# Late attention as one run of products per tile, with a compact state, in a fused attention, gate and expert kernel

## The chip, the cores and the metric

One core of one Trainium2 chip runs the kernel. The metric is the device time of one execution in microseconds; three runs of the kernel before gave 864.8 to 867.6, with a median of 867.41. A difference under about 0.3% (2.6 us) can't be told from none.

## The reference

Three parts follow one another. The sizes are 4 batches, 8 heads, 768 steps, head width 64; 3072 tokens of width 512; 768 columns in the first expert layer; 8 experts of 1024 columns.

```python
gamma = 1.0 - 2.0 ** (-5.0 - np.arange(H))
for t in range(S):                                    # attention: a decaying state per head
    state = gamma * state + outer(k[t], v[t])
    y[t] = q[t] @ state / sqrt(D)
h = np.maximum(np.maximum(x @ w1, x @ w2), x @ w3)    # x: all tokens, heads side by side
x = h @ w_out
logits = x @ w_gate                                   # each expert takes its 384 best tokens
out[mask_e] = np.maximum(x[mask_e] @ w1[e], 0) @ w2[e]
```

## The kernel before

Attention works on 24 tiles of 128 steps. `ORDER` goes through the batches first, so four neighbouring tiles are one block of 512 tokens, and there are six blocks. Within a tile the recurrence is written as products: scores (keys by queries, `pa`, `scores`, L216), masked on VectorE into `at` (L230); the state by the queries into `px` (L242); keys by values into `pp`, which is added to the state (L247, L259); values by masked scores into `px` as well (L250). ScalarE copies `px` into `xhi`, rounded to a shorter format, and VectorE puts the rest into `xlo` (L260, L261), so that later products are made of three products in that format. `visit` (L232) does this for tile t and calls `scores` for tile t+1 at its end.

Heads lie in pairs: heads 2j and 2j+1 share one product's 128 rows. The state is a tile of 128 by 4 by 128 per batch, with the two heads' 64 by 64 squares on the diagonal and zeros beside them, cleared by GpSimd at the start (L408); its product has all 128 rows and columns, four of them per tile.

`att_front` (L176) brings a tile there: SP loads queries, keys and values (`load_tile`, two tiles ahead), GpSimd multiplies in the decay (L186), and then queries and keys are transposed. For the first eight tiles (`DIRECT = 8`) TensorE does that (L194). For the late ones VectorE transposes squares of 32 by 32 (`blocks`, L204), and SP moves them out to memory and back in place (`there`, L206, and `qk`, L208); ScalarE then copies the keys to `kT` (L212). The buffers of `qk` are two, so the way back for tile t+2 begins when tile t's products have read theirs.

`moe1` (L347) makes the wide products `pm` of 128 by 512 (L358): for each of 18 groups (six parts of the columns, three matrices) twelve products, and ScalarE or VectorE takes the maximum into `hb`. `logits` (L372) multiplies `hb` by the product of the output and gate weights, 24 products of 32 columns per block, in three runs of 16, 4 and 4 products. These have the bank `pl`, `px` has one, the wide products three, and the pool `att` three.

All of it is written as generators. `interleave` (L110) advances the attention of the next block by so many steps per step of `moe1`; a late tile's front has five yields. A scheduler then orders each engine's instructions along these lines, so the order on the chip is close to that of the code, not equal to it. In the first part of the program block 0 and block 1 go through the first matrix alone, while the weights of the others are loaded and decoded from 64-bit numbers on VectorE (`decode`, L291 to L295), rounded on ScalarE (L309) and split on GpSimd (L310). After the sixth block the tokens are multiplied by the output weights (`x2`, L485) while the routing is worked out, and then the eight experts run (L801, L814); their products `py` alternate between the banks `px` and `pl`.

Of the kernel before, what the change touches and what calls it, by code (L numbers as in the profile page):

```python
# [23 lines left out]
P = 128  # L24
# [102 lines left out]
HALF = (slice(0, 64), slice(64, 128))  # L127


class Kernel:  # L130
    def __init__(self, ctx, tc, q, k, v, w1, w2, w3, w_out, w_gate, e1, e2, ca, cr, out):
# [17 lines left out]
        self.tiles, self.fronts, self.ats = {}, {}, {}  # L149
# [4 lines left out]
    def bank(self, tag, shape, bufs, name):  # L154
        return self.ps.tile(shape, F32, tag=tag, name=name, bufs=bufs)
# [10 lines left out]
    def load_tile(self, t):  # L166
        if t >= NT or t in self.tiles:
            return
        b, c = ORDER[t]
        self.tiles[t] = []  # L170
        for n, src, bufs in (("q", self.q, 2), ("k", self.k, 4), ("v", self.v, 4)):
            x = self.sp.tile([P, H, D], F32, tag="in_" + n, name="in_" + n, bufs=bufs)
            self.nc.sync.dma_start(x, src[b, :, c * P:(c + 1) * P, :].rearrange("h t d -> t h d"))
            self.tiles[t].append(x)

    def att_front(self, t):  # L176

# [6 lines left out]
        of_tile = lambda n: ca[:, CA["t" + n]].rearrange("p (c h) -> p c h", h=H)[:, ORDER[t][1]]  # L184
        for n, x in (("q", qn), ("k", kn)):
            nc.gpsimd.tensor_tensor(x, x, of_tile(n).unsqueeze(2).to_broadcast([P, H, D]), op=OP.mult)  # L186
# [28 lines left out]

    def scores(self, t):  # L216
# [5 lines left out]
        for j in range(4):  # L222
            for g in range(2):
                nc.tensor.matmul(pa[g][:, j].rearrange("p (b i) -> p b i", b=4),
                                 kT[HALF[g], j].rearrange("p b i -> p (b i)"), qT[HALF[g], :, j, :],
                                 start=j == 0, stop=True, skip_group_check=True)
        mask = self.ca[:, CA["mask"]].unsqueeze(1).to_broadcast([P, 4, P])
        self.ats[t] = [self.ap.tile([P, 4, P], F32, tag="at", name="at") for _ in range(2)]
# [3 lines left out]
    def visit(self, t, xhi, xlo, off):  # L232
# [6 lines left out]
        px = self.bank("px", [P, 4, P], 1, "px")  # L239
        if c > 0:  # L240
            for j in range(4):
                nc.tensor.matmul(px[:, j, :].rearrange("p (b i) -> p b i", b=4), state[:, j, :], qT[:, :, j, :],  # L242
                                 start=j == 0, stop=False, skip_group_check=True)
        if c < CPB - 1:
            pp = self.bank("att", [P, 4, 64], 3, "pp")
            for h in range(H):
                nc.tensor.matmul(pp[HALF[h % 2], h // 2, :], ks[:, h, :], vt[:, h, :], start=h < 2, stop=True,  # L247
                                 skip_group_check=True)
        for h in range(H):
            nc.tensor.matmul(px[HALF[h % 2], h // 2, :], vt[:, h, :], at[h % 2][:, h // 2, :],  # L250
                             start=c == 0 and h < 2, stop=True, skip_group_check=True)
# [8 lines left out]
        nc.scalar.copy(xhi[:, :, off:off + P], px)  # L260
        nc.vector.tensor_tensor(xlo[:, :, off:off + P], px, xhi[:, :, off:off + P].bitcast(F32), op=OP.subtract)  # L261

    def att_block(self, i, x):
        if i == 0:
            yield from self.att_front(0)
            yield from self.att_front(1)
            self.scores(0)
            yield
        for b in range(B):
            t = i * B + b  # L270
            self.visit(t, *x, b * P)
            if t + 2 < NT:
# [74 lines left out]
    def moe1(self, i, x, hb, only=None, tail=None):  # L347
# [5 lines left out]
        for n, (f, w) in enumerate(groups):  # L353
# [13 lines left out]
            if tail and n in (12, 13, 16):  # L367
                next(tail)
# [3 lines left out]
    def logits(self, i, hb):  # L372
# [3 lines left out]
        pl = self.bank("pl", [P, B, 32], 1, "pl")  # L376
# [7 lines left out]
        yield  # L384
        for f in range(4):
            product(f)
        yield
        product(4)
        yield
        product(5)  # L390
# [5 lines left out]
    def phase_ab(self, ctx_h):  # L396
# [3 lines left out]
        with ExitStack() as ctx:  # L400
# [20 lines left out]
            fill = chain(self.att_block(2, xn), self.logits(0, hbs[0]))  # L421
            interleave(self.moe1(1, x, hbs[1], only=(1, 2)), fill, 24 / 24)
            for i in range(2, NB):
                x, hbs[i] = xn, new_h()
                fill, tail = [], None
                if i + 1 < NB:
                    xn = new_x()
                    fill.append(self.att_block(i + 1, xn))
                else:
                    tail = self.logits(i, hbs[i])  # L430
                fill = chain(*fill, self.logits(i - 1, hbs[i - 1]))
                interleave(self.moe1(i, x, hbs[i], tail=tail), fill, 24 / 36)
# [357 lines left out]
    def ffn(self, e):  # L790
# [16 lines left out]
        for g in range(3):  # L807
            py = self.bank(("px", "pl")[g % 2], [P, DM], 1, "py")
# [82 lines left out]
```

## Time and profile before

| | us |
|---|---|
| median of three runs | 867.41 |
| the profiled execution, its own time | 867.75 |
| its span, first to last instruction | 866.0 |
| TensorE busy | 830.4 (96%) |
| VectorE busy | 412.4 (48%) |
| ScalarE busy | 224.2 (26%) |
| GpSimd busy | 271.8 (31%) |
| wide products of `moe1` (L358), 1296 | 518.8 |

TensorE's busy time is a union of the products' durations, which overlap: a wide product is listed with 0.40 us, though the next one starts about 0.23 after it. A busy engine in this sense is one that always has a product under way, and its price per product is the distance between starts. A product in the 32-bit format leaves two records in the trace, one in the shorter format a single record. The granted clock of TensorE is 1.00 at 2.4 GHz and 0.50 at 1.2 GHz; its mean over the span is 0.978.

### The profile page before, as it was taken

The numbers are of one execution on the slowest core, as the hardware profiler recorded it, in microseconds if no ns is written. First come the engines' busy times: TensorE is split into PE (matmuls) and PEld (weight loads), VectorE is DVE, ScalarE is ACT, GpSimd is POOL, SyncE is SP. The second block draws the span as 40 slices with busy tenths as digits, with TensorE's granted clock in tenths as the row PEclk, the third lists the DMA queues.
The fourth block names the chain that finished last, engine by engine and source line by source line (L and its number), as shares of the span: only waits on it lengthen the run. The fifth ranks groups of instructions, "written<-read, shape, count | busy, mean of one in ns | idle before, by whom it ended". The sixth has DMA issues, their size and how long they took to land. (4 is left out here: it accounts for less than half of the span.)

```text
span 866.0 us, 13113 instructions
## 1 busy us (share of the span) xinstructions
PE 830.4 (96%) x5210; PEld 692.1 (80%) x5210; DVE 412.4 (48%) x727; ACT 224.2 (26%) x360; POOL 271.8 (31%) x275
## 2 busy tenths in 40 slices
PE   7997999999999999999999999989899998989997
PEld 6775888878878878877777777678789888888996
DVE  3687483544334322231149766746355544446310
ACT  3433211101111111211024223144244433344210
POOL 5565031111110100002026555356444743515001
PEclk9898999999999999999999999999899999989999
DMA  9979485657446413100037654149657756452000
GB/s 221 208 193 222 128 262 175 159 171 169 111 133 170 134 38 124 47 27 1 1 115 251 206 169 149 50 124 229 149 150 200 179 164 179 129 171 67 13 24 37
DMA packets 129342, 118.02 MB, mean 136 GB/s; under 512 B 82048, under 2 KB 106752, under 8 KB 128256
## 3 DMA queue, kind: packets, MB, share of 16 engines
q1 hardware_dynamic: 123232, 96.54, 41.5%
q0 software_dynamic: 5328, 14.16, 5.3%
q10 hardware_dynamic: 720, 6.47, 1.9%
q8 instruction: 41, 0.67, 0.3%
q14 instruction: 21, 0.17, 0.1%
HBM read 88.30 MB, written 28.84 MB: 135 GB/s over the span
## 5 line engine op out<-in xcount | busy, mean ns | idle before, releaser
L358 PE MATMUL pm<-xhi,whi 128*128 128x512 f32 x432 | 176.2, 409 | 5.3 <-ACT xhi L260 5.3
L358 PE MATMUL pm<-xlo,whi 128*128 128x512 f32 x432 | 171.3, 397 | 0.5 <-DVE xlo L261 0.5
L358 PE MATMUL pm<-xhi,wlo 128*128 128x512 f32 x432 | 171.3, 396 | 0.0
L762 POOL DMA_INDIRECT xg<-x_rows,idx x87 | 95.7, 1100 | 102.8 <-DVE xt L777 69.7
L365 DVE TENSOR_TENSOR hb<-hb,pm 128x512 f32<-128x512 f32 x72 | 49.5, 687 | 163.1 <-PE pm L358 160.0
L462 POOL TENSOR_TENSOR hsl<-hb,hsh 128x256 fp32r<-128x256 f32 x72 | 61.6, 886 | 152.8 <-ACT hsh L460 149.6
L358 PEld LDWEIGHTS pm<-xhi,whi 128*128 128x128 f32 x432 | 81.8, 190 | 28.3 <-ACT xhi L260 5.5
L750 DVE TENSOR_TENSOR elo<-eraw,ehi 128x1024 fp32r<-128x1024 f32 x64 | 78.9, 1245 | 41.6 <-ACT ehi L749 23.6
L358 PEld LDWEIGHTS pm<-xhi,wlo 128*128 128x128 f32 x432 | 81.5, 189 | 19.1
L358 PEld LDWEIGHTS pm<-xlo,whi 128*128 128x128 f32 x432 | 81.6, 189 | 18.6 <-DVE xlo L261 1.4
L801 PE MATMUL ph<-xtlo,ehi 128*128 128x384 f32 x256 | 88.8, 347 | 5.3 <-issue 5.2
L801 PE MATMUL ph<-xthi,ehi 128*128 128x384 f32 x256 | 89.2, 350 | 2.7 <-issue 1.6
L801 PE MATMUL ph<-xthi,elo 128*128 128x384 f32 x256 | 88.5, 346 | 1.8 <-issue 1.7
L749 ACT CAST ehi<-eraw 128x1024 fp32r<-128x1024 f32 x64 | 65.7, 1049 | 45.4 <-PE py L814 18.1
L814 PE MATMUL py<-elo,hhi 128*128 128x512 f32 x192 | 74.9, 390 | 0.0
L814 PE MATMUL py<-ehi,hlo 128*128 128x512 f32 x192 | 74.8, 390 | 0.0
L814 PE MATMUL py<-ehi,hhi 128*128 128x512 f32 x192 | 74.7, 389 | 0.0
L805 DVE SCALAR_TENSOR_TENSOR hlo<-ph,hhi 128x384 fp32r<-128x384 f32 x64 | 35.3, 555 | 59.2 <-ACT hhi L804 54.4
L485 PE MATMUL px<-wohi,hsh 128*128 128x512 f32 x144 | 58.8, 408 | 0.6 <-PEq L593 0.6
L363 ACT COPY hb<-pm 128x512 f32<-128x512 f32 x36 | 21.1, 587 | 147.0 <-PE pm L358 147.0
L186 POOL TENSOR_TENSOR in_k<-in_k,ca 128x512 f32<-128x512 f32 x24 | 26.2, 1093 | 102.6 <-DMA in_k<-in_k_dram 90.0
L485 PE MATMUL px<-wolo,hsh 128*128 128x512 f32 x144 | 57.0, 396 | 0.0
(155 smaller groups left out, 1189.3 us busy)
## 6 DMA issues: line engine op xcount, KB each, us to landing
eraw<-in_moe_w_dram SPq DMA_DIRECT2D x36, 512.0 KB
eraw<-in_moe_w_dram SPq DMA_DIRECT2D x112, 128.0 KB
w<-in_moe_w_dram SPq DMA_DIRECT2D x24, 384.0 KB
there<-blocks SPq DMA_DIRECT2D x16, 512.0 KB
qk<-there SPq DMA_DIRECT2D x64, 128.0 KB
in_q<-in_q_dram SPq DMA_DIRECT2D x24, 256.0 KB
in_k<-in_k_dram SPq DMA_DIRECT2D x24, 256.0 KB
in_v<-in_v_dram SPq DMA_DIRECT2D x24, 256.0 KB
```

Source lines behind the costliest of these rows:

```text
L186: nc.gpsimd.tensor_tensor(x, x, of_tile(n).unsqueeze(2).to_broadcast([P, H, D]), op=OP.mult)
L358: nc.tensor.matmul(pm, a[w][kt][:, f * P:(f + 1) * P], xx[:, kt, :], start=m == 0, stop=m == 3 * KD - 1)
L363: nc.scalar.copy(hb[:, f, :], pm)
L365: nc.vector.tensor_tensor(hb[:, f, :], hb[:, f, :], pm, op=OP.max)
L462: nc.gpsimd.tensor_tensor(lo[:, f:f + 2, :], hb[:, f:f + 2, c * P:(c + 1) * P], hi[:, f:f + 2, :].bitcast(F32), op=OP.subtract)
L485: nc.tensor.matmul(pm, a[:, f, :], self.wo[f][b], start=m == 0, stop=m == 3 * NF - 1)
L749: nc.scalar.copy(hi, raw)
L750: nc.vector.tensor_tensor(lo, raw, hi.bitcast(F32), op=OP.subtract)
L762: nc.gpsimd.indirect_dma_start(out=x[:, b * P:(b + 1) * P] if e else x, out_offset=None, in_=self.x2_rows.rearrange("n (r c) -> (n r) c", ...
L801: mm = nc.tensor.matmul(pm, a[:, kt, :], x[:, kt, :], start=m == 0, stop=m == 3 * KD - 1)
L805: nc.vector.scalar_tensor_tensor(hlo[f], pm, 0.0, hhi[f].bitcast(F32), op0=OP.max, op1=OP.subtract)
L814: mm = nc.tensor.matmul(py, a[:, s], b, start=m == 0, stop=m == 3 * KF2 - 1)
```

## The change

- The state becomes 128 by 4 by 64 per batch: the heads are paired as j and j+4, one in the upper and one in the lower 64 rows, and there are no zeros to clear. Its product is eight products of 64 rows by 64 columns; `px` has two banks, one for each half of the rows, and `pl` goes. Logits take a bank of `att`; so do the experts' `py`.
- From tile 8 on a visit begins with the scores of the next tile, and all its products are tied in the written order (`follow`). In the early tiles the scores still end the visit.
- The logits of blocks 0 to 4 are one run of 24 products, for blocks 0 to 3 right behind the second visit of a block.
- Of tile 8's front only the first step is done between the visits of tiles 6 and 7; its transposes, its scores and then tile 9's front follow tile 7's visit.
- The steps per step of `moe1` are 20 for 24 or 36 instead of 24.
- Queries and keys of the first eight tiles are loaded in two halves of the heads; late transposes on VectorE come in four halves instead of two.

```diff
-    def keep_warm(self, x, n, tag="pl"):
+    def keep_warm(self, x, n, tag="px"):
...
+            if n != "v" and t < DIRECT:
+                for g in range(2):
+                    self.nc.sync.dma_start(x.rearrange("p (j g) d -> p g j d", g=2)[:, g], src[:, 4 * g:4 * g + 4])
...
-                nc.vector.transpose(blocks[:, :, n], x.rearrange("p h d -> p (h d)").rearrange("p (j r d) -> p r j d", j=4, r=4))
+                x = x.rearrange("p (r j) (e d) -> p r e j d", r=2, e=2)
+                for r in range(2):
+                    nc.vector.transpose(blocks[:, 2 * r:2 * r + 2, n], x[:, r])
...
+    def follow(self, mm):
+        if self.behind:
+            self.tc.add_manual_dep(mm.ins, self.behind.name, NEXT, reason="kinds of products together")
+        self.behind = mm.ins
...
-        px = self.bank("px", [P, 4, P], 1, "px")
+        px = self.ps.tile([P, 2, 512], F32, tag="px", name="px", bufs=1)[:, :, :2 * P]
+        out = lambda h: px[HALF[h % 2], h // 4, h % 4 // 2 * P:(h % 4 // 2 + 1) * P]
+        steady, ahead = t >= DIRECT, t + 1 in self.fronts
+        self.behind = None
+        if steady and ahead:
+            self.scores(t + 1)
         if c > 0:
-            for j in range(4):
-                nc.tensor.matmul(px[:, j, :].rearrange("p (b i) -> p b i", b=4), state[:, j, :], qT[:, :, j, :],
-                                 start=j == 0, stop=False, skip_group_check=True)
+            for h in (0, 4, 1, 5, 2, 6, 3, 7):
+                g, j = h // 4, h % 4
+                self.follow(nc.tensor.matmul(out(h).rearrange("p (b i) -> p b i", b=4), state[HALF[g], j, :],
+                                             qT[HALF[g], :, j, :], start=j < 2, stop=True, skip_group_check=True))
...
-        if t + 1 in self.fronts:
+        if not steady and ahead:
             self.scores(t + 1)
-        if c < CPB - 1:
-            for r in HALF:
-                if c == 0:
-                    nc.scalar.copy(state[r, :, r], pp[r])
-                else:
-                    nc.vector.tensor_tensor(state[r, :, r], pp[r], state[r, :, r], op=OP.add)
+        if c == 0:
+            nc.scalar.copy(state, pp)
+        elif c < CPB - 1:
+            nc.vector.tensor_tensor(state, pp, state, op=OP.add)
...
-    def att_block(self, i, x):
+    def att_block(self, i, x, beside=None, at=1):
...
+            self.visit(t, x, b * P)
+            if beside and b == at:
+                for _ in beside:
+                    pass
+            if t == DIRECT - 2:
+                first = self.att_front(t + 2)
+                next(first)
+                yield
+            elif t == DIRECT - 1:
+                yield from first
+                self.scores(t + 1)
+                self.behind = None
+                yield from self.att_front(t + 2)
...
-        pl = self.bank("pl", [P, B, 32], 1, "pl")
+        pl = self.bank("att", [P, B, 32], 3, "pl")
...
-            self.states = [self.wp.tile([P, 4, P], F32, name=f"state{b}") for b in range(B)]
-            for state in self.states:
-                nc.gpsimd.memset(state, 0.0)
+            self.states = [self.wp.tile([P, 4, 64], F32, name=f"state{b}") for b in range(B)]
...
-            fill = chain(self.att_block(2, xn), self.logits(0, hbs[0]))
-            interleave(self.moe1(1, x, hbs[1], only=(1, 2)), fill, 24 / 24)
+            fill = self.att_block(2, xn, self.logits(0, hbs[0]))
+            interleave(self.moe1(1, x, hbs[1], only=(1, 2)), fill, 20 / 24)
...
-            py = self.bank(("px", "pl")[g % 2], [P, DM], 1, "py")
+            py = self.bank("att", [P, DM], 3, "py")
```

How the order of the instructions changes is shown at three places. In these rows the first word is the line of the code, `x8` says that eight such instructions follow one another, and the sizes are those of the output. The first place is TensorE around the visit of tile 9 (its state is `state_158`; L242, L247, L250 and L224 are state, keys by values, values by scores, and scores of tile 10). Before:

```order
L358 MATMUL pm<-xlo,whi_583 128x512
L358 MATMUL pm<-xhi,wlo_587 128x512
L242 MATMUL px<-qk,state_158 128x128 x4
L247 MATMUL pp<-in_v,in_k 64x64 x8
L250 MATMUL px<-at,in_v 64x128 x8
L224 MATMUL pa<-qk,kT 128x128 x8
L358 MATMUL pm<-xhi,whi_580 128x512
```

Now (L245, L271, L276, L279, and L425 for the logits, which before stood elsewhere in three runs):

```order
L403 MATMUL pm<-xlo,whi_589 128x512
L403 MATMUL pm<-xhi,wlo_593 128x512
L245 MATMUL pa<-qk,kT 128x128 x8
L271 MATMUL px<-qk,state_158 64x128 x8
L276 MATMUL pp<-in_v,in_k 64x64 x8
L279 MATMUL px<-at,in_v 64x128 x8
L425 MATMUL pl<-hb,wpr 32x128 x24
L403 MATMUL pm<-xhi,whi_586 128x512
```

The scores went from the end of the run to its start, the state's products are eight of half the rows and half the columns, and block 0's logits follow the visit in one run.

The second place is TensorE around the visit of tile 7 (`state_160`), the last tile of block 1. Before, the wide products behind it are already block 1's, which need this tile:

```order
L358 MATMUL pm<-xlo,whi_244 128x512
L358 MATMUL pm<-xhi,wlo_248 128x512
L242 MATMUL px<-qk,state_160 128x128 x4
L247 MATMUL pp<-in_v,in_k 64x64 x8
L250 MATMUL px<-at,in_v 64x128 x8
L358 MATMUL pm<-xhi,whi_241 128x512 x3
```

Now the wide products within the visit, and 16 behind it, are still block 0's:

```order
L271 MATMUL px<-qk,state_160 64x128 x8
L276 MATMUL pp<-in_v,in_k 64x64 x8
L279 MATMUL px<-at,in_v 64x128 x2
L403 MATMUL pm<-xhi,whi_243 128x512
L403 MATMUL pm<-xlo,whi_243 128x512
L403 MATMUL pm<-xhi,wlo_247 128x512
L403 MATMUL pm<-xhi,whi_244 128x512
L403 MATMUL pm<-xlo,whi_244 128x512
L403 MATMUL pm<-xhi,wlo_248 128x512
L403 MATMUL pm<-xhi,whi_245 128x512
L403 MATMUL pm<-xlo,whi_245 128x512
L279 MATMUL px<-at,in_v 64x128 x6
```

The visit moved ahead by 16 wide products, and eight more split its last kind, of which the first two need the first half of the mask and the six behind them the second.

The third place is VectorE at the same visit, from the first half of tile 7's mask on. `w` is a raw piece of weights, `wbits` its decoded form. Before:

```order
L230 TENSOR_TENSOR at<-pa,ca 128x512
L295 SCALAR_TENSOR_TENSOR wbits<-w_719,wbits 128x384
L291 TENSOR_SCALAR wbits<-w_721 128x384
L230 TENSOR_TENSOR at<-pa,ca 128x512
L293 SCALAR_TENSOR_TENSOR wbits<-w_721,wbits 128x384
L204 STREAM_TRANSPOSE blocks<-in_k 128x4x128
L295 SCALAR_TENSOR_TENSOR wbits<-w_721,wbits 128x384
L291 TENSOR_SCALAR wbits<-w_800 128x384
```

Now (piece 730 answers to 719 before, 732 to 721):

```order
L251 TENSOR_TENSOR at<-pa,ca 128x512
L338 SCALAR_TENSOR_TENSOR wbits<-w_703,wbits 128x384
L336 TENSOR_SCALAR wbits<-w_730 128x384
L340 SCALAR_TENSOR_TENSOR wbits<-w_703,wbits 128x384
L336 TENSOR_SCALAR wbits<-w_732 128x384
L338 SCALAR_TENSOR_TENSOR wbits<-w_730,wbits 128x384
L338 SCALAR_TENSOR_TENSOR wbits<-w_732,wbits 128x384
L340 SCALAR_TENSOR_TENSOR wbits<-w_730,wbits 128x384
L340 SCALAR_TENSOR_TENSOR wbits<-w_732,wbits 128x384
L251 TENSOR_TENSOR at<-pa,ca 128x512
L287 TENSOR_TENSOR state_160<-pp,state_160 128x256
L219 STREAM_TRANSPOSE blocks<-in_q 128x2x128
```

All of the decoding of pieces 730 and 732 now stands ahead of the second half of the mask, where before two steps of the last piece stood behind it; the first half of the mask stands further ahead.

## Rows read from the trace of the kernel before

**Rows 1.** Stretches: length, PE, PEld, DVE, ACT, POOL busy, PE clock, DMA share, GB/s.

```profile
0.00:70.00 70.00, 62.23 (x612) 52.38 (x614) 46.40 (x78) 27.05 (x52) 38.80 (x42) 0.95 0.89 202
...
77.00:84.00 7.00, 6.52 (x20) 4.67 (x21) 4.99 (x8) 1.62 (x3) 5.02 (x5) 0.70 1.19 261
...
95.00:139.00 44.00, 43.96 (x236) 35.93 (x234) 29.71 (x49) 7.53 (x17) 12.59 (x15) 1.00 0.60 177
139.00:444.00 305.00, 305.00 (x2113) 245.17 (x2112) 101.57 (x170) 37.94 (x64) 29.51 (x33) 1.00 0.37 100
```

**Rows 2.** TensorE's timeline at tile 9: start, duration, line, names, records.

```profile
151.45 1.05 PE L242 MATMUL px<-qk,state 128*128 128x128 f32 x8
152.44 0.69 PE L247 MATMUL pp<-in_v,in_k 128*64 128x64 f32 x16
152.95 1.05 PE L250 MATMUL px<-at,in_v 128*64 128x128 f32 x16
153.93 1.16 PE L224 MATMUL pa<-qk,kT 64*128 64x128 f32 x16
155.02 0.51 PE L358 MATMUL pm<-xhi,whi 128*128 128x512 f32 x1
...
162.10 0.38 PE L242 MATMUL px<-qk,state 128*128 128x128 f32 x2
```

**Rows 3.** TensorE's timeline at block 0's logits.

```profile
184.88 1.08 PE L380 MATMUL pl<-hb,wpr 128*32 128x128 f32 x32
185.90 0.50 PE L358 MATMUL pm<-xhi,whi 128*128 128x512 f32 x1
...
187.47 0.43 PE L380 MATMUL pl<-hb,wpr 128*32 128x128 f32 x8
187.83 0.50 PE L358 MATMUL pm<-xhi,whi 128*128 128x512 f32 x1
```

**Rows 4.** TensorE's timeline, second and last of 36 wide products between logits.

```profile
431.24 0.51 PE L358 MATMUL pm<-xhi,whi 128*128 128x512 f32 x1
431.58 0.39 PE L358 MATMUL pm<-xlo,whi 128*128 128x512 f32 x1
...
439.49 0.40 PE L358 MATMUL pm<-xhi,wlo 128*128 128x512 f32 x1
439.81 0.43 PE L380 MATMUL pl<-hb,wpr 128*32 128x128 f32 x8
```

**Rows 5.** TensorE's timeline at tile 20, whose visit has no keys by values.

```profile
328.20 1.09 PE L250 MATMUL px<-at,in_v 128*64 128x128 f32 x16
329.23 0.49 PE L224 MATMUL pa<-qk,kT 64*128 64x128 f32 x4
```

**Rows 6.** TensorE's timeline behind tile 7's visit.

```profile
76.75 1.65 PE L358 MATMUL pm<-xhi,whi 128*128 128x512 f32 x3 [5.27 <-ACT xhi L260]
78.88 0.80 PE L358 MATMUL pm<-xlo,whi 128*128 128x512 f32 x1 [0.48 <-DVE xlo L261]
```

**Rows 7.** ScalarE's timeline: the split of tile 7.

```profile
76.12 0.58 ACT L260 CAST xhi<-px 128x512 fp32r<-128x512 f32 x1
```

**Rows 8.** VectorE's timeline around tile 7.

```profile
61.89 0.43 DVE L259 TENSOR_TENSOR state<-pp,state 64x256 f32<-64x256 f32 x1
...
68.50 0.68 DVE L230 TENSOR_TENSOR at<-pa,ca 128x512 f32<-128x512 f32 x1
69.10 1.24 DVE L293 SCALAR_TENSOR_TENSOR wbits<-w,wbits 128x384 int32<-128x384 int32 x1
70.26 0.70 DVE L204 STREAM_TRANSPOSE blocks<-in_k 128x512 f32<-128x512 f32 x1
70.89 0.51 DVE L295 SCALAR_TENSOR_TENSOR wbits<-w,wbits 128x384 int32<-128x384 int32 x1
...
78.13 0.69 DVE L261 TENSOR_TENSOR xlo<-px,xhi 128x512 fp32r<-128x512 f32 x1
```

**Rows 9.** ScalarE's timeline: keys of tile 10 come back from memory.

```profile
149.17 0.62 ACT L212 COPY kT<-qk 128x512 f32<-128x512 f32 x1 [5.18 <-DMA qk<-there]
```

More of the change, by code (lines that the diff above doesn't have):

```diff
@@ L148, in __init__ @@
         self.wo_rows = self.dp.tile([FF, DM], F32, name="wo_rows")
-        self.tiles, self.fronts, self.ats = {}, {}, {}
+        self.tiles, self.fronts, self.ats, self.behind = {}, {}, {}, None
         self.zeros = self.cp.tile([P, P], BF16, name="zeros")
@@ L154, in bank @@
     def bank(self, tag, shape, bufs, name):
+        if tag == "px":
+            return self.ps.tile([P, 2, 512], F32, tag=tag, name=name, bufs=1)[:, 0, :shape[1]]
         return self.ps.tile(shape, F32, tag=tag, name=name, bufs=bufs)
-    def keep_warm(self, x, n, tag="pl"):
+    def keep_warm(self, x, n, tag="px"):
         pw = self.bank(tag, [P, 512], 1, "warm")
@@ L223, in scores, with visit @@
             for g in range(2):
-                nc.tensor.matmul(pa[g][:, j].rearrange("p (b i) -> p b i", b=4),
-                                 kT[HALF[g], j].rearrange("p b i -> p (b i)"), qT[HALF[g], :, j, :],
-                                 start=j == 0, stop=True, skip_group_check=True)
+                self.follow(nc.tensor.matmul(
+                    pa[g][:, j].rearrange("p (b i) -> p b i", b=4), kT[HALF[g], j].rearrange("p b i -> p (b i)"),
+                    qT[HALF[g], :, j, :], start=j == 0, stop=True, skip_group_check=True))
         mask = self.ca[:, CA["mask"]].unsqueeze(1).to_broadcast([P, 4, P])
-        self.ats[t] = [self.ap.tile([P, 4, P], F32, tag="at", name="at") for _ in range(2)]
+        self.ats[t] = [self.ap.tile([P, 4, P], F32, tag="at", name="at", bufs=4) for _ in range(2)]
         for at, p in zip(self.ats[t], pa):
             nc.vector.tensor_tensor(at, p, mask, op=OP.mult)
-    def visit(self, t, xhi, xlo, off):
+    def visit(self, t, x, off):
         nc = self.nc
@@ new lines, in visit @@
+        for h in (0, 1, 4, 5, 2, 3, 6, 7):
+            self.follow(nc.tensor.matmul(out(h), vt[:, h, :], at[h // 4][:, h % 4, :], start=c == 0 and h % 4 < 2, stop=True,
+                                         skip_group_check=True))
+        if not steady and ahead:
+            self.scores(t + 1)
+        self.behind = None
[3 more added lines that the diff above has]
+            nc.vector.tensor_tensor(state, pp, state, op=OP.add)
+        px = px.rearrange("p g (j i) -> p g j i", j=2)
@@ L264, in att_block @@
+        xhi, xlo = [a[:, :, off:off + P].rearrange("p (g j) i -> p g j i", g=2) for a in x]
+        nc.scalar.copy(xhi, px)
+        nc.vector.tensor_tensor(xlo, px, xhi.bitcast(F32), op=OP.subtract)
+    def att_block(self, i, x, beside=None, at=1):
         if i == 0:
@@ L267, in att_block @@
             self.scores(0)
+            self.behind = None
             yield
@@ L270, in att_block @@
             t = i * B + b
-            self.visit(t, *x, b * P)
-            if t + 2 < NT:
+            self.visit(t, x, b * P)
[9 more added lines that the diff above has]
+                self.scores(t + 1)
+                self.behind = None
+                yield from self.att_front(t + 2)
+            elif t + 2 < NT:
                 yield from self.att_front(t + 2)
@@ L367, in moe1, with logits @@
             if tail and n in (12, 13, 16):
-                next(tail)
+                next(tail, None)
         if i < NB - KEPT and (only is None or 2 in only):
             nc.scalar.dma_start(self.h_rows[i], hb)
-    def logits(self, i, hb):
+    def logits(self, i, hb, stops=()):
         nc = self.nc
-        pl = self.bank("pl", [P, B, 32], 1, "pl")
+        pl = self.bank("att", [P, B, 32], 3, "pl")
         def product(f):
@@ L382, in product @@
                                  skip_group_check=True)
-        yield
-        for f in range(4):
+        for f in range(NF):
+            if f in stops:
+                yield
             product(f)
[L387 to L390, printed above, removed]
         lt = self.lp.tile([P, B, 32], F32, tag="lt", name="lt")
```

33 lines of the change are left out of this document (17 added, 16 removed).

## The prediction

> **What bounds the kernel now.** I read the busy time by stretch first, because a share over the whole span hides which stage is full. In the stretch from 139 to 444 us TensorE is busy for 305.00 of 305.00 us at the full clock of 2.4 GHz, with VectorE at 101.6 and the DMA engines at 0.37 [rows 1]. Nothing is waited for there: what TensorE issues is what the stretch lasts, and a microsecond of issue saved is a microsecond of the end. From 95 to 139 it is busy for 43.96 of 44. Only the first 77 us have holes. Second I read TensorE's timeline, by start times: the duration of a product there overlaps with the next one, so the price of a run is the distance from its start to that of the next kind. Third, VectorE's and ScalarE's timelines at tile 7, where the largest hole lies.
>
> **One late visit.** Before, tile 9 takes from 151.45 to 155.02, that is 3.57 us: the old state's product 0.99 (8 records for 4 products), keys by values 0.51, scores by values 0.98, scores of the next tile 1.09 [rows 2]. To this comes what a change of the array's shape costs the wide products around it. Wide products start every 0.2326 us (34 steps from the second to the 36th in 7.91 us) [rows 4]; 30 of them between two visits take 7.08, 0.10 over 30 times the pitch [rows 2], and 36 between two pieces of the logits 8.57, 0.20 over [rows 4]. So 0.10 is the first wide product behind a narrow run, and the other 0.10 is the entry from a wide product into a narrow shape. The old state product has the wide shape, so a visit enters free; now it begins with the scores, which fill half the rows, and pays. Before: 3.57 + 0.10 = 3.67.
>
> The state product is now eight products of 64 rows by 64 columns, 16 records in four quarters of the array. No row of the trace has that shape. The bounds: with two at a time it is what scores by values take for as many records, 0.98 [rows 2]; with four at a time it is the logits' price, which put four products side by side: 32 records take 1.02 and 8 take 0.36, or 0.0275 a record, so 16 take 0.58 [rows 3]. I take 0.58, since the row halves (scores) and the column quarters (logits) overlap each by itself and the new order goes round the quarters. It also changes shape twice inside narrow runs instead of once; such a change shows as 0.05 more, 1.03 for scores by values right behind the state product at tile 20 [rows 5] against 0.98 behind keys by values [rows 2]. After: 0.10 + 1.09 + 0.05 + 0.58 + 0.51 + 0.98 + 0.10 = 3.41, which is 0.26 less. Sixteen visits (tiles 8 to 23): **4.2 us**. On the price of overlap the Trainium skill (TensorE: Matmul & The Clock Gate, "Measured speedup vs the span model") says that each further tile of the array adds some 4 ns to one product; four rounds would then take about 0.48 and 16 visits 1.6 us less still, an estimate by that page that no row here shows and the sum does not use. The same notes speak against the change elsewhere (TensorEngine Tiling, "Key Properties"): another tiling mode drains the engine. The 0.10 and 0.05 above are what such a change costs in this trace, and the visit has one more of them now.
>
> **The logits.** Before, a block's logits are three runs of 32, 8 and 8 records with wide products between: 1.02 + 0.36 + 0.36, an entry of 0.10 and a first wide product of 0.10, and 0.17 for each stretch between (six wide products take 1.57, their pitch is 1.40) [rows 3]: 2.28. Now 48 records stand in one run, 1.02 + 16 x 0.0275 = 1.46. Behind a visit (blocks 0 to 3) they pay only a change of 0.05, so 0.77 less each; block 4's stand alone, 1.46 + 0.20, 0.62 less. Block 5's keep their three stops. Together **3.7 us**.
>
> **Tile 7.** Before, tile 7's visit comes when all 72 wide products of block 0's first matrix are done. The next wide product needs that tile: it starts at 76.75 after an idle 5.27, released by ScalarE's split, and another waits 0.48 more for VectorE's [rows 6]. The split itself is short; it stood in ScalarE's queue behind casts of decoded weights until 76.12 [rows 7], and VectorE's half behind the decoding until 78.13 [rows 8]. In the change tile 7's visit comes four steps earlier, and the order of TensorE puts 16 wide products of block 0 behind it. They cover the split. What is late next is the second half of tile 7's masked scores: it started at 68.50 before and now has two decoding steps more ahead of it (1.24 and 0.51), and fewer: three second halves of a state sum at 0.43 and half of a transpose of 0.70 [rows 8]. That gives 68.6 to start; VectorE is at work nearly all the time there, yet every earlier TensorE step gives it some of its idle time back, so I take 68.6 for its end, 0.7 earlier. Then six products by values (0.73 at 0.061 a record), 0.10, and 16 x 0.2326 = 3.72: block 1's first wide product at 73.2 instead of 76.75, and no wait of 0.48, since VectorE needs behind the mask one state sum, three half transposes, a decode step and the split, 2.6 to 3.6 us, against 4.6 on TensorE. Gain **4.1 us**. Ends: the mask no earlier, 3.4; VectorE quick enough that it is not waited for, 6.2. The clock was at 0.70 on the mean from 77 to 84 us [rows 1], so for 4.2 us it ran at 1.2 GHz, behind that idle time, and lost 2.1. A wait of some 3 us for the mask stays, so I count no gain of clock; the other end is 2.1.
>
> **What costs nothing.** Late transposes on VectorE come in four halves instead of two of 0.70 [rows 8], between 0 and 1.4 us more per tile, 22 at most; 139 to 444 has 203 idle [rows 1]. Of 16 more load issues on SP in the first 62 us (queries and keys of tiles 0 to 7 in two halves) the bytes are the same, and the DMA engines are at 0.89 there [rows 1], so bytes set the pace; without that cover each would delay the loads behind it. GpSimd's four clears of the state and ScalarE's second state copies go, beside longer waits. The products y alternate over three banks of the common pool instead of two of their own, with one bank more to evacuate. SP's transpose loads wait for the state product (it reads the last of a tile), now 1.2 us later in the run. Before, keys of tile 10 were ready at 149.79 [rows 9], 1.66 ahead of tile 9's visit; the visit is now 36 products behind the last instead of 30, 1.4 later, so the slack stays at about 1.9, and more where 54 lie between. Behind 444 us nothing changes place; it moves as a whole.
>
> **The sum.** 4.2 + 3.7 + 4.1 = 12.0 us. The profiled execution took 867.75 for a span of 866.0, 0.3 over the median of 867.41; from the median this gives **855.4 us**.
>
> **The rivals.** (a) The hole at tile 7 stays: VectorE decodes at its pace, the new order only moves the wait from the split to the mask, and block 1 starts at 76.75 again. For it speaks how full VectorE is; against it that 24 wide products now stand where TensorE stood still. Only 7.9 are gained: 859.5. (b) The quarters run only two at a time, since every quarter shares its rows with one and its columns with another. The state run takes 0.98, each late visit 0.40 more: 855.4 + 6.4 = 861.8. Against it: both kinds of sharing overlap by themselves. (c) Slower: quarters don't overlap at all. Then 16 records at the 0.124 of the old run take 1.98, 1.40 over my price, 22.4 in all: 877.8. It turns into a loss from 1.33 us a run on (12.0 over 16, plus 0.58). No row speaks for it, none excludes it. (d) The scores, now first in the run, wait for their keys: each microsecond by which these come late is paid at 15 visits, so that 0.8 eats the gain and 1.0 gives 855.4 + 15 = 870.4. The slack of 1.9 stands against it.
>
> **How the numbers follow.** The forecast, with the ends above (the clock kept, no wait at the mask, a cheaper or dearer change of shape), spans 849 to 858.5 and gets 0.62; (a) 0.17, (b) 0.13, (c) 0.04, (d) 0.04. The range from 848.5 to 862 takes in the first three and leaves out (c), (d) and the cases where (a) and (b) meet. A measurement of this kernel can tell about 0.3%, 2.6 us. Faster by more than that are the forecast, (a) and (b) but for the 0.04 in which they add up to nothing: 0.88. Within it that 0.04 and half of (d): 0.06. Slower: 0.06.
>
> **What would show it.** In the profile after: 16 state records from start to next kind in 0.55 to 0.65, a run from scores to the next wide product in 3.3; 48 logits records in 1.4 to 1.5 right behind a visit; TensorE full from 95 to the end of the blocks, and that stretch shorter by 8; block 1's first wide product at 72 to 74 us, behind a wait of about 3 us inside tile 7's visit. A state run of 0.9 or more is (b) or (c); an idle TensorE ahead of the scores, released by keys, is (d); block 1's start at 76 or later is (a). Wrong altogether would be a stretch behind 444 us that changes its length by more than 2 us.

## The result, and the profile after

The changed kernel takes **853.7 us** (median of four runs, 852.3 to 860.6) beside 867.5 for the kernel before on the same chip: ratio **0.9877**, 95% interval 0.984 to 0.991. (The quotient of the two medians is 0.984, at the edge of that interval.) Run again later, beside other kernels, it gave 0.9843 (0.980 to 0.988). The forecast was 855.4 us in a range of 848.5 to 862. The profiled execution took 852.29 us for a span of 850.5.

Stretches of the profile after, with the columns of [rows 1], the last two cut at about the same work:

```profile
77.00:84.00 7.00, 7.00 (x32) 5.63 (x31) 6.14 (x8) 2.49 (x5) 5.96 (x6) 1.00 1.15 262
...
92.50:136.00 43.50, 42.79 (x233) 35.55 (x233) 30.85 (x54) 7.10 (x17) 13.81 (x15) 1.00 0.65 194
136.00:430.00 294.00, 294.00 (x2230) 235.41 (x2230) 97.53 (x180) 37.47 (x63) 28.56 (x32) 1.00 0.39 103
```

The late stretch is as full as before, 294.00 of 294.00 us, so all that it lost was issue. From 92.5 to 136 us TensorE is busy for 42.79 of 43.50: it stands idle for 0.71 us ahead of the gate's first transposes, where it had waited 0.03, a loss that the forecast did not have. From 77 to 84 us the granted clock is 1.00, which is 2.4 GHz, where it was 0.70 [rows 1]: this the forecast had not counted.

TensorE's timeline after at tile 9 and block 0's logits (start, duration, line, names, records):

```profile
149.30 1.16 PE L245 MATMUL pa<-qk,kT 64*128 64x128 f32 x16
150.39 0.67 PE L271 MATMUL px<-qk,state 64*64 64x128 f32 x16
150.99 0.69 PE L276 MATMUL pp<-in_v,in_k 128*64 128x64 f32 x16
151.51 1.05 PE L279 MATMUL px<-at,in_v 128*64 128x128 f32 x16
152.48 1.52 PE L425 MATMUL pl<-hb,wpr 128*32 128x128 f32 x48
153.93 0.50 PE L403 MATMUL pm<-xhi,whi 128*128 128x512 f32 x1
```

From start to start: scores 1.09, state 0.60 (0.98 to 0.99 before [rows 2]), keys by values 0.52, scores by values 0.97, logits 1.45. The visit takes 3.18, and nothing waits for its keys.

TensorE's timeline at tile 7, first the start of its visit before, behind all 72 wide products of block 0's first matrix, then the visit after:

```profile
68.94 1.05 PE L242 MATMUL px<-qk,state 128*128 128x128 f32 x8
```

```profile
65.61 0.44 PE L279 MATMUL px<-at,in_v 128*64 128x128 f32 x4 [0.28 <-DVE at L251]
...
69.55 0.88 PE L279 MATMUL px<-at,in_v 128*64 128x128 f32 x12 [1.45 <-DVE at L251]
70.36 0.50 PE L403 MATMUL pm<-xhi,wlo 128*128 128x512 f32 x1
...
74.19 0.40 PE L403 MATMUL pm<-xhi,whi 128*128 128x512 f32 x1
```

Two of the products by values (four records) come with the first half of the mask, eight wide products follow, then TensorE waits 1.45 us for the second half. The 16 wide products from 70.36 are block 0's last; the 17th, at 74.19, is block 1's first (76.75 before [rows 6]). VectorE's rows name what it did between the halves (the last four of eight decoding operations, then the mask):

```profile
66.95 1.01 DVE L338 SCALAR_TENSOR_TENSOR wbits<-w,wbits 128x384 int32<-128x384 int32 x2
67.89 1.01 DVE L340 SCALAR_TENSOR_TENSOR wbits<-w,wbits 128x384 int32<-128x384 int32 x2
68.83 0.67 DVE L251 TENSOR_TENSOR at<-pa,ca 128x512 f32<-128x512 f32 x1
```

For a yardstick that leaves out the start (the first wide product began between 35.2 and 38.9 us in these executions) and the experts, I use the time from TensorE's first wide product to the first of x2. Kernel before, then after:

```profile
35.49 0.49 PE L358 MATMUL pm<-xhi,whi 128*128 128x512 f32 x1
...
443.05 0.39 PE L485 MATMUL px<-wohi,hsh 128*128 128x512 f32 x1
```

```profile
36.28 0.49 PE L403 MATMUL pm<-xhi,whi 128*128 128x512 f32 x1
...
429.44 0.39 PE L525 MATMUL px<-wohi,hsh 128*128 128x512 f32 x1
```

That is **407.56 before and 393.16 after, 14.4 us less**; below it is called the middle. From x2's first product to the end of the span it is 422.95 before and 421.06 after. The middle repeats well: it is 392.99 to 393.71 us in three traces of the change (two of its own, one with another order of the heads) and 407.56 and 408.69 in two that leave it as before.

The forecast also named the stretch behind tile 7. From the scores of tile 8 to x2's first product:

```profile
95.30 1.16 PE L224 MATMUL pa<-qk,kT 64*128 64x128 f32 x16
```

```profile
92.48 1.16 PE L245 MATMUL pa<-qk,kT 64*128 64x128 f32 x16
```

It lasts 347.75 us before and 336.96 after. Ten wide products (2.3 us) have moved ahead of it, so 8.5 are gained there; the forecast's first two terms are 7.9.

### The profile page after: what moved, and what is told of

Its sections match the earlier page's. It is cut to its first block, busy times and chain, and to the rows that moved or that the text cites. A ratio compares the mean times of both kernels' runs of the same rounds, so it can differ in the third digit from the quotient of the medians.

```text
span 850.5 us, 13474 instructions
## 1 busy us (share of the span) xinstructions
PE 816.5 (96%) x5370; PEld 675.9 (79%) x5370; DVE 412.2 (48%) x743; ACT 223.4 (26%) x356; POOL 275.7 (32%) x271
## 5 line engine op out<-in xcount | busy, mean ns | idle before, releaser
L403 PE MATMUL pm<-xhi,whi 128*128 128x512 f32 x432 | 173.8, 402 | 0.0
L802 POOL DMA_INDIRECT xg<-x_rows,idx x87 | 98.1, 1127 | 103.3 <-DVE xt L817 68.4
L525 PE MATMUL px<-wohi,hsl 128*128 128x512 f32 x144 | 56.7, 394 | 0.0
```

What stands on the lines that cost most here:

```text
L403: nc.tensor.matmul(pm, a[w][kt][:, f * P:(f + 1) * P], xx[:, kt, :], start=m == 0, stop=m == 3 * KD - 1)
L525: nc.tensor.matmul(pm, a[:, f, :], self.wo[f][b], start=m == 0, stop=m == 3 * NF - 1)
L802: nc.gpsimd.indirect_dma_start(out=x[:, b * P:(b + 1) * P] if e else x, out_offset=None, in_=self.x2_rows.rearrange("n (r c) -> (n r) c", ...
```

## Experiments

The kernel before took 850.8, 850.8 and 864.3 us in the three comparisons that follow, on three chips; so only ratios to it and rows are compared.

### The three terms, undone one at a time

**Tiles 7 and 8 in the old order**, all else as changed:

```diff
-            if t == DIRECT - 2:
...
-            elif t == DIRECT - 1:
...
-            elif t + 2 < NT:
+            if t + 2 < NT:
```

> The change without its reordering at tiles 7 and 8: tile 8's transposes and tile 9's follow their visits as in the kernel before. Theory (the idle time at tile 7 comes from the order in which TensorE takes visit 7 and block 0's last products): the hole of some 5 us is there again, block 1's first wide product at 76 to 77 us instead of 74.1, and behind it some microseconds at the lower clock; 4.1 us more than the change by the forecast's term, 5 to 6 with the clock: 858 to 860 us, ratio to the kernel before 0.992. Rival (the hole went because VectorE is less busy there, with halved transposes and a compact state sum): block 1 still starts near 74.1 us and the time stays within 1 us of 853.7.

Ratio 0.9937 (0.991 to 0.996). TensorE at tile 7, and the stretch behind:

```profile
70.95 1.39 PE L279 MATMUL px<-at,in_v 128*64 128x128 f32 x16
75.11 0.97 PE L403 MATMUL pm<-xhi,whi 128*128 128x512 f32 x3 [2.78 <-ACT xhi L290]
79.21 0.79 PE L403 MATMUL pm<-xlo,whi 128*128 128x512 f32 x1 [3.12 <-DVE xlo L291]
```

```profile
77.00:84.00 7.00, 4.79 (x13) 3.85 (x14) 6.12 (x11) 1.22 (x3) 4.89 (x6) 0.57 1.19 265
```

The hole is back: 5.90 us idle against 1.73 in the change, now more behind VectorE's half of the split than ScalarE's. With it comes the low clock, 0.57. The middle lasts 399.80 us (36.49 to 436.29), **6.6 more** than in the change. The rival falls: the compact state and the halved transposes do not close the hole.

**Logits in three runs** behind the last visit:

```diff
-            fill = self.att_block(2, xn, self.logits(0, hbs[0]))
+            fill = chain(self.att_block(2, xn), self.logits(0, hbs[0], (0, 4, 5)))
```

(and the same for the later blocks, with the old pace of 24 steps)

> The change with every block's logits in three runs of 32, 8 and 8 records behind the last visit, as in the kernel before. Theory (each split costs two changes of the array's shape and the fill between): 0.77 us more for blocks 0 to 3 and 0.62 for block 4, 3.7 us more than the change: 857.4 us, ratio to the kernel before 0.992; 0.62 to 0.82 us per block in the rows of TensorE. Rival (the logits' price is in their 48 records, wherever they stand, and the stretches between cost nothing): under 1 us more.

Ratio 0.9936 (0.991 to 0.996). Block 0's logits:

```profile
181.01 1.08 PE L425 MATMUL pl<-hb,wpr 128*32 128x128 f32 x32
182.02 0.50 PE L403 MATMUL pm<-xhi,whi 128*128 128x512 f32 x1
...
183.62 0.42 PE L425 MATMUL pl<-hb,wpr 128*32 128x128 f32 x8
183.97 0.50 PE L403 MATMUL pm<-xhi,whi 128*128 128x512 f32 x1
```

They repeat [rows 3]: 1.01, 0.35 and, further on, 0.35 again. The middle lasts 396.48 (38.94 to 435.42), **3.3 more** than in the change. The ratio says 5 us, but with an interval of about 2.5 us to each side and the change's own 3 us, so it does not contradict the rows.

**Both undone**: what is left is the compact state, the scores at the head, halved transposes and y's banks.

> The change with both the logits in three runs and the order of tiles 7 and 8 as before: what is left of it is the compact state with the scores at the head of the late visits, the halved transposes and y's banks. Theory (the three terms add up): the forecast's first term alone, 4.2 us, ratio to the kernel before 0.995; between TensorE's first wide product and x2's first 4 to 5 us less than in the kernel before (407.6 us), so 402.6 to 403.6. Rival (the terms interact, or a fourth gain of 3 us or more lies in what the forecast costed at nothing): 0.991 or less. Other rival (the compact state brings nothing that the end sees): 0.998 or more.

Ratio 0.9968 (0.9945 to 0.9991). The middle: 

```profile
38.08 0.50 PE L403 MATMUL pm<-xhi,whi 128*128 128x512 f32 x1
...
441.81 0.39 PE L525 MATMUL px<-wohi,hsh 128*128 128x512 f32 x1
```

403.73, **3.8 less** than before, though TensorE stands idle 1.39 us here ahead of the gate's first transposes (0.03 before). So 3.8 + 3.3 + 6.6 = 13.7 of the 14.4 us: the terms add up nearly, and no fourth one of 3 us is hidden. The ratio alone does not exclude the rival's 0.998; the middle does.

**The order of tiles 7 and 8 put alone into the kernel before:**

> The kernel before with the reordering at tiles 7 and 8 alone: block-diagonal state, logits in three runs, transposes unsplit. Theory (the order alone closes the hole): it brings what taking it back cost in the trace of the run before this one, 6.6 us between TensorE's first wide product and x2's first: ratio to the kernel before 0.992, block 1's first wide product at 73 to 75 us. Rival (it needs the compact state sum and the halved transposes, which make VectorE quicker at tile 7): the wait for the mask grows by 1 to 2 us and under 4 us are gained, ratio 0.9955 or more.

Ratio 0.994 (0.992 to 0.996), 5.1 us of 850.8 with an interval from 3.7 to 6.5. The middle:

```profile
38.71 0.49 PE L367 MATMUL pm<-xhi,whi 128*128 128x512 f32 x1
...
442.92 0.39 PE L494 MATMUL px<-wohi,hsh 128*128 128x512 f32 x1
```

It lasts 404.21, which is 3.4 us less than in the kernel before, and 4.5 less than the 408.69 of a run on the same chip whose middle is as before (y over three banks, below). By the rows this is less than the 6.6 that undoing the order cost, and the rival's "under 4 us" is not excluded. TensorE still waits 1.23, 0.88 and 0.28 us inside tile 7's visit and stands idle for 1.35 ahead of the gate's first transposes (at 114.68 us). The order alone brings half of the gain or more; how much of the rest needs the compact state and the halved transposes stays open.

### Why a state run takes 0.6 us

**Same quarter twice in a row** (one line: the heads' order).

```diff
-            for h in (0, 4, 1, 5, 2, 6, 3, 7):
+            for h in (0, 2, 4, 6, 1, 3, 5, 7):
```

> The eight state products of a visit are issued in another order, two in the same quarter of the array behind each other, the rest as in the change. Theory (products overlap when they lie in different quarters, and issue is in order): of the eight only the second of one quarter and the first of the next can run together, so a run goes in five steps instead of two. At 0.245 us a step (the pairs of scores by values, 0.98 for four steps) a state run takes 1.22 us instead of 0.598, that is 0.62 more, 16 times where TensorE is full: about 10 us more than the change, 863.5 us, ratio to the kernel before 0.995. Rival one (quarters never overlap, the run is short only because its weights are half as wide): it stays at 0.6 and the time at 853.7. Rival two (the order breaks every overlap): 8 steps, 1.98 us, 22 us more, 876 us.

**In pairs of row halves**, (0, 4, 2, 6, 1, 5, 3, 7):

> The state products go in pairs: the two row halves of the array in the same column half behind each other, so that only two at a time can run side by side. Theory (it was four at a time that made the run 0.598 us): four steps of 0.245 us, 0.98 us a run, 0.38 more for 16 late visits, 6.1 us more than the change: 860 us, ratio to the kernel before about 0.9915. Rival (two at a time is all that the array gives, in any order): the run stays at about 0.6 us and the time at 853.7, ratio 0.988. This is the forecast's rival (b), made on purpose.

Ratios 0.987 (0.983 to 0.991) and 0.985 (0.982 to 0.989): both as fast as the change. TensorE's rows at tile 9, of the one and of the other:

```profile
150.81 0.69 PE L271 MATMUL px<-qk,state 64*64 64x128 f32 x16
151.43 0.69 PE L276 MATMUL pp<-in_v,in_k 128*64 128x64 f32 x16
```

```profile
154.67 0.68 PE L271 MATMUL px<-qk,state 64*64 64x128 f32 x16
155.28 0.69 PE L276 MATMUL pp<-in_v,in_k 128*64 128x64 f32 x16
```

0.62 and 0.61 us instead of 0.60. My theory fell: the order in which the quarters follow one another costs next to nothing. Left were a narrow product that is cheap by itself, and quarters that overlap whatever their order. Two kernels decide, by sending the same 16 records to fewer quarters.

```diff
-                self.follow(nc.tensor.matmul(out(h).rearrange("p (b i) -> p b i", b=4), state[HALF[g], j, :],
-                                             qT[HALF[g], :, j, :], start=j < 2, stop=True, skip_group_check=True))
+                self.follow(nc.tensor.matmul(out(h - h % 2).rearrange("p (b i) -> p b i", b=4), state[HALF[0], j, :],
+                                             qT[HALF[0], :, j, :], start=j == 0, stop=True, skip_group_check=True))
...
```

The second kernel keeps `HALF[g]`. In both, the products by values get another `start` flag.

> All eight state products of a visit are issued in one and the same quarter of the array (rows 0 to 63, columns 0 to 63), so that none can overlap another; this leaves out what the other three quarters compute, the second half of each tile's state among it. Theory (the 0.598 us of a state run come from quarters that run side by side, with products of a quarter queued far enough ahead that their order does not matter): 16 records one behind the other at the 0.123 us of the old run's records, 1.97 us a run, 1.37 more, 22 us in all. Rival (a product of half the rows and half the columns is simply cheaper, and quarters have no part in it): the run stays at 0.6 us and the time where the change has it. Between them, about 1.0 us, only two would run side by side in the change.

> The eight state products go into two quarters of the array only, its two row halves in the first column half, alternating; this leaves out what the second column half computes. Theory (one quarter took 1.887 us, four take 0.598): two quarters, each with half of the single quarter's queue, take about half of it, 0.94 to 1.0 us. Rival (the four do not share evenly, two row halves at a time are what overlaps and columns bring nothing): 0.6 us as with four. Other rival (only column halves overlap): 1.9 us.

One quarter, then two:

```profile
158.19 1.96 PE L271 MATMUL px<-qk,state 64*64 64x128 f32 x16
160.08 0.69 PE L276 MATMUL pp<-in_v,in_k 128*64 128x64 f32 x16
```

```profile
155.64 1.09 PE L271 MATMUL px<-qk,state 64*64 64x128 f32 x16
156.66 0.69 PE L276 MATMUL pp<-in_v,in_k 128*64 128x64 f32 x16
```

1.89 us in one quarter, 1.02 in two, 0.60 in four. Quarters do run side by side, and the run lasts as long as its fullest quarter: about 0.11 us a record there, plus 0.15. The Trainium skill (TensorE: Matmul & The Clock Gate, "Part 3: Packing small matmuls — row/col tiling") calls products strict FIFO in start and end. If one that finds its quarter taken held up those behind it, the first order would have cost five steps, 1.2 us; it measured 0.62, so no such hold-up is seen here, and in the starts of single records the trace does not agree. The records under way in the first tenth of a microsecond of a state run (in brackets), in one quarter, then in the first order:

```profile
158.18:158.28 0.10, 0.09 (x1) 0.09 (x2) 1.00 0.00 0
```

```profile
150.80:150.90 0.10, 0.09 (x4) 0.09 (x7) 1.00 0.00 0
```

One quarter starts one record in that time. The first order starts four, though in the written order the first four records all belong to one quarter: records of later products have started ahead of the first quarter's second one.

### What the head of the visit and y's banks are worth

**Scores last again in a late visit**, the state product compact:

```diff
-        if steady and ahead:
+        if False:
...
-        if not steady and ahead:
+        if ahead:
```

> The change with the scores of the next tile at the end of a late visit instead of its head; all else as in the change. Theory (the state product now has a narrow shape, so whichever product comes first pays the entry from a wide one, 0.10 us): a late visit from its first narrow product to the next wide one lasts as long as in the change, 3.18 us, within 0.05; the time is within 2 us of the change, ratio to the kernel before 0.988. Rival (the head of the run matters: the wait for the state product's operands, or a dearer change of shape behind a wide product): 0.2 us or more a visit, 3 us in all.

Ratio 0.991 (0.989 to 0.994). A late visit, then the same trace at tile 7:

```profile
153.49 0.67 PE L271 MATMUL px<-qk,state 64*64 64x128 f32 x16
...
156.67 1.52 PE L425 MATMUL pl<-hb,wpr 128*32 128x128 f32 x48
```

```profile
72.29 0.88 PE L279 MATMUL px<-at,in_v 128*64 128x128 f32 x12 [3.09 <-DVE at L251]
73.09 0.66 PE L403 MATMUL pm<-xhi,wlo 128*128 128x512 f32 x1
73.55 0.63 PE L403 MATMUL pm<-xhi,whi 128*128 128x512 f32 x1
73.97 0.63 PE L403 MATMUL pm<-xlo,whi 128*128 128x512 f32 x1
```

```profile
73.00:80.00 7.00, 7.00 (x27) 5.55 (x24) 6.87 (x13) 2.82 (x6) 3.18 (x4) 0.76 0.91 213
```

The visit is 3.18 us in either order, as the theory had it, and 36 wide products between two visits take 8.56 to 8.58 us in both, 0.20 over 36 times the pitch: the entry is paid once, whichever narrow product comes first. Still its middle is 3.0 us longer than the change's, 396.16. This lies ahead of tile 8, in code that the edit leaves alone: the wait for tile 7's mask is 3.09 us here, and behind it wide products start every 0.43 us and not every 0.23 (granted clock 0.76 in that stretch). VectorE's rows say why:

```profile
68.97 2.66 DVE L340 SCALAR_TENSOR_TENSOR wbits<-w,wbits 128x384 int32<-128x384 int32 x2
71.56 0.68 DVE L251 TENSOR_TENSOR at<-pa,ca 128x512 f32<-128x512 f32 x1
```

The two decoding operations that took 1.01 us in the change take 2.66. Six traces have this order at tile 7 and the state in four quarters (the change twice, the two head orders, the logits apart, and this). Four waited 1.44 to 1.45 us and kept the full clock; two waited 3.09 and 3.10 (this one and the row pairs) and lost it, at a price of 1.5 us (94 wide products from there in 23.59 against 22.12). The middle of the row pairs, 396.36, is 3.2 longer too, which the ratio 0.985 does not show. In all six a product of GpSimd starts 0.43 or 0.44 us behind the first of the last four decoding operations; it takes 2.38 us in the four and 1.43 or 1.44 in the two. The change's own kernel had the short wait in both of its traces; whether the length belongs to the kernel or to the execution stays open.

**y over three banks**, in the kernel before:

```diff
-            py = self.bank(("px", "pl")[g % 2], [P, DM], 1, "py")
+            py = self.bank("att", [P, DM], 3, "py")
```

> The kernel before with one edit of the experts alone: the products y go over the three banks of the common pool instead of alternating over two of their own. Theory (costed at nothing in the forecast): ratio to the kernel before 1.000, within 0.3%. Rival (the evacuation of y was waited for, and part of the gain of the change lies here): the stretch from the experts' first product to the end is 2 us or more shorter, ratio 0.997 or less.

Ratio 1.002 (1.001 to 1.004): no gain in it, as costed. From the experts' first product to the end its trace takes 266.7 us, against 267.9 in the one on the same chip with two banks (the order put alone), short of the rival's 2 us.

### Can the last wait go?

**Attention's step ahead of the decoding's** in block 1, `(a, b)` for `(b, a)` in `zip_gens`, and the change itself beside it:

> The changed kernel once more, beside the next one: ratio to the kernel before 0.985 to 0.991. In its trace the wait for the second half of tile 7's mask should be between 1.4 us (the change's first trace) and 3.1 us (the run with the scores last), by when the weights that VectorE decodes ahead of it arrive; the state runs 0.598 and the logits 1.447 as before. Nothing in the forecast needs this run but as a yardstick on one chip.

> The change with each step of block 1's attention issued ahead of that step's weight decoding instead of behind it, so that of the seven decoding operations between the two halves of tile 7's mask one is left. Theory (the wait of TensorE for the second half is VectorE's queue, and decoding can wait): the 1.4 to 3.1 us go, block 1's first wide product comes 1.5 to 3 us earlier and the time is 1.5 to 3 us under the change, ratio to the kernel before 0.002 to 0.0035 lower than the change beside it. Rival (the decoded weights are due: TensorE waits for ScalarE's casts or for the gate's first transposes instead): the wait moves to 105 to 112 us, or the GpSimd queue delays tile 8, and the time is the same or up to 2 us more.

The change: 0.984 (0.980 to 0.988), its wait 1.44. The new order: **0.989** (0.985 to 0.993), 4.3 us slower than the change beside it by the medians and 4.2 by the middle (397.15 against 392.99).

```profile
65.31 0.82 PE L271 MATMUL px<-qk,state 64*64 64x128 f32 x16 [1.93 <-DVE xlo L291]
...
68.47 0.70 PE L279 MATMUL px<-at,in_v 128*64 128x128 f32 x4 [1.28 <-DVE at L251]
```

One decoding operation is left between the halves of the mask (of eight, not seven as written above), but others now lie ahead of tile 6's split and of the mask's first half. Tile 7's visit needs the bank that this split frees and waits 1.93 us for it, then 1.28 for the mask, and loses the clock (0.58 on the mean from 70 to 77 us). The wait moved forward, which neither theory had named. Nothing that ran beats the change.

## Why the prediction was right, point by point

- **What bounds it.** TensorE's issue, stretch by stretch. It held: the middle shrank by 14.4 us with TensorE as full as before, but for 0.71 us ahead of the gate's transposes, which the forecast put at nothing.
- **One late visit**, forecast 3.41 from entry to first wide product, 0.26 less. Measured 3.18 + 0.20 = 3.38, 0.29 less, 4.6 over 16 visits by the rows; 3.8 in the kernel that has little else, its longer idle time included. Term 4.2: right. Its reason for 0.58 was half wrong. "The new order goes round the quarters" is not what makes it so; that the load is spread over four quarters is. The 0.48 given beside the sum was 0.12 short. Rival (b) is dead by the 0.60 itself, and the row pairs, which were meant to bring it about, did not. Rival (c) is dead too; only its price for one quarter was near, 1.98 against 1.89.
- **The entry of 0.10**, taken from 0.20 that wide products lost around a narrow run: the visit with the scores last and the same 8.57 us behind it bear it out.
- **The logits**, 3.7: 3.3 by the run that splits them again. One run of 48 records takes 1.45, forecast 1.46.
- **Tile 7**, 4.1: 6.6, the term that was mis-sized. Its mechanism stood: 16 products cover the split, and the mask's second half is late next. It began at 68.83, where the working had it start at 68.6. The step that failed is "I count no gain of clock". It rested on a wait of some 3 us staying; the wait was 1.45, and the clock did not fall. The forecast's own figures did not give 3: the old visit's start, 68.94, moved ahead by 24 wide products (5.6), with 0.1 for the entry, 0.58, 0.51 and 0.24 for its products and 2.1 for the eight wide ones, has TensorE through at 66.9; the mask's end was put at 68.6, so 1.7 was to be expected. Undoing the order costs 4.2 us of idle time and, by its 22.07 us from 75.11 to tile 8's scores for 72 wide products (16.75 at their pitch, 3.12 idle), 2.2 of clock; the forecast had that 2.1 as an end of its range.
- **Rival (a)**, the hole moves to the mask, was half right. A wait of 3.1, as forecast, did occur in two of six traces and cost clock again; there the gain is 3.0 to 3.2 smaller. Block 1's first wide product is the 73rd of all; it starts 41.3 us behind the first one in the kernel before, 37.3 to 38.1 behind it in the four traces with the short wait, and 41.0 in the two with the long one, as (a) had it. But (a) priced that at no gain, and some 3.5 us are left: before, TensorE went on to lose 2.7 us behind that start (68 products in 18.55 us, 15.8 at their pitch), and now that loss lies ahead of it. Which of the two waits a trace has, no term of the forecast tells.
- **Keys late**, rival (d): TensorE waits nowhere from 136 to 430 us, and ahead of that from 92.5 us on only for the gate's transposes, so 15 visits pay nothing.
- **What costs nothing.** y's banks and VectorE's halved transposes: nothing seen, though the transposes were not tried alone. Nor were the halved loads; the first wide product began at 36.3 to 38.9 us with halves and at 35.2 to 38.7 without, too scattered to tell.
- **Behind x2's first product** it forecast no change of over 2 us, and 1.9 was seen. In the other traces, with the same products there and on other chips too, this stretch took 404 to 424 us, so that bound tells less than it seemed to.
- **The sum**: 12.0 forecast; 13.8 by the medians, 10.7 by the ratio (7.5 to 13.9), 14.4 in the middle of the two traces. The whole times cannot tell 12 from 14. By the rows, what was missing is the clock at tile 7.

## What to carry to other kernels

Where one engine issues without a gap, price each run from its start to the next kind's start, with the first product behind it; such terms added up here to within a microsecond. Small products gain when their records are spread over all quarters of the array; their order within a run was free here. And where an edit closes a hole on TensorE, count with it the slow products that follow the hole, and carry them as a bound of their own: the length of a wait alone did not tell here whether they would come.

## What the runs showed of the hardware that was not expected

- Sixteen records of 64 by 64 cost 1.89, 1.02 and 0.60 us in one, two and four quarters; two neighbours in one quarter cost 0.02 more in a run.
- At tile 7 the granted clock stayed at 1.00 behind waits of 1.44 and 1.45 us and fell to 0.50 behind 3.09 and 3.10. The length of the last wait does not decide it alone. It fell behind 1.93 us (attention's step first) and behind 1.37 (state in one quarter), and stayed at 1.00 behind 2.13 with two more waits of 0.59 and 0.88 (state in two quarters). One quarter, then two, with the stretch around:

```profile
67.83 2.69 PE L271 MATMUL px<-qk,state 64*64 64x128 f32 x16 [1.37 <-DVE xlo L291]
70.00:77.00 7.00, 6.75 (x45) 5.07 (x44) 6.97 (x15) 1.78 (x5) 3.78 (x4) 0.59 0.75 184
```

```profile
68.58 1.09 PE L271 MATMUL px<-qk,state 64*64 64x128 f32 x16 [2.13 <-DVE xlo L291]
63.00:77.00 14.00, 10.40 (x102) 8.06 (x98) 13.93 (x28) 4.12 (x8) 8.04 (x8) 1.00 0.75 201
```

- One and the same decoding operation (L340, 128x384) took 0.54 us, or 1.33 each as a pair. In the slow case (68.97 to 71.56 us in the run with the scores last) GpSimd's products lie beside it the whole time; in the change, where a GpSimd product lay beside the same pair, that product took 2.38 us instead of 1.4 and the pair 0.54 each. The Trainium skill (GPSIMD Engine Reference, "1. Specifications") names contention with VectorE's operations that read two inputs from SBUF, which fits. That it sets the length of the wait at tile 7 goes with all six traces, two long and four short, and was not tested.
